# Zero halves for q and v in the first batch of a banded attention with a gated feed-forward, and its buffers moved

## Chip, cores and metric

The kernel runs on one core of one Trainium2 chip. The metric is the device time of one execution in microseconds (us), as a median of three runs. An execution that the hardware profiler took supplies the rows below.

## What is computed

Four batches, eight heads, 768 positions, head size 64. Attention looks at a window of 128 positions back and at 4 sink positions; its output, 3072 tokens of 512 features, goes through a gated feed-forward (512 to 1536 to 512):

```python
scores = scale * np.matmul(q, k.transpose(0, 1, 3, 2))
rel = pos[:, None] - pos[None, :]
in_window = (rel >= 0) & (rel < int(window))
keep = (pos[None, :] < int(n_sink)) | in_window
scores = np.where(keep, scores, -1000000000.0)
a = softmax(scores)                       # over the last axis
x = (a @ v), heads side by side           # 3072 x 512
gate = 1.0 / (1.0 + np.exp(-(x @ w_gate)))
return (gate * (x @ w_val)) @ w_out
```

All in 32-bit floats. The weights come in as 64-bit floats and are turned into two fp32r parts (high and low) on the chip.

## The kernel before, in words

**Units.** Attention works in units: one head and one group of 128-row query tiles. Batch 0 has two groups of three tiles (T = 3), so units u = 0 to 7 (group 1) and 8 to 15 (group 2); batches 1 to 3 have three groups of two tiles. Units of three tiles are called plain: scores and P times v are one fp32 matmul each (two records and four passes of the array), while T = 2 units split into fp32r parts.

**A plain unit** (`attend`, L795). Loads of k, q and v (`load`, L768); for each tile a score matmul (`qk`), a mask and row maximum on VectorE (`top`), an exponential with row sums on ScalarE; then row sums and their reciprocal (`guard`), normalisation of P on GpSimd, ScalarE or VectorE, a copy of the sink columns into `psk`, three transposes on TensorE, a copy into `wt` (the turned weights), two selects on GpSimd that cut the window's triangles, and P times v (`pv`) into one bank `xr` for a pair of heads, even head on partitions 0 to 63, odd head on 64 to 127. When both are done ScalarE copies the bank into `xs`.

**Half arrays.** From unit `DUP = 4` on, q and k of a pair of heads are loaded once, one head on the upper and one on the lower 64 partitions, and a score matmul contracts over 64 rows (`rows = slice(e, e + D)`). Units 0 to 3 load q and k of one head twice, on both halves, and contract over 128 rows with half the scale. P times v of all plain units uses 64 columns of the array (`vhl()[:, l]` is 64 wide).

**Join** (L1046). After unit 7 (and 15) the sink columns are turned, copied and split into `sk`, multiplied with sink values `vsp` in four matmuls, added onto `xs` by VectorE, and written as the high and low parts `XH` and `XL`, which the feed-forward reads.

**Feed** (L1215). Tokens go in eight chunks of three tiles. For each of twelve slices f of the hidden size: 24 matmuls of 384 columns (`m`, gate and value, in program order over all f and chunks), tanh on ScalarE, product and split on VectorE, ScalarE and GpSimd, nine matmuls of 512 columns into `o0` to `o2`.

**Weights** (`decode`, L1119; `weights`, L1172). Each f needs three matrices, each loaded through a staging buffer `wst` (three of them), decoded on ScalarE and VectorE, and kept. f0 is opened by the row sums of unit 1, f1 to f11 by those of unit 7 (`GATES`, `OPEN`).

**Shared places.** `wst1` and `wst2` hold P, v and one `wt` of early units (u < 8, `EP`, `EV`, `EW`) and serve as staging only after these are done (`plan.over`). `eq` tiles in a pool "early" hold q and k for some of the first four units; later tiles of T = 2 units (`qs`, `kh`, `vhl`) take that place. The score banks of early units (`eO`) are the banks that become `o0` to `o2`; other PSUM uses share three banks `a`.

**Order.** Every operation goes through `plan.op` with a priority (u for attention; 6 + 0.3n for the n-th decoded matrix; behind all for the feed's matmuls on TensorE; ahead of all for the feed's other work), candidates of engines and estimated durations. `Plan.run` simulates and fixes the order of each engine, SP's transfer queue included. When TensorE has nothing, it puts a fill (`warm`, a 128 x 128 matmul on the identity), always before 8.5 us and later only if the estimated share of busy time of late, weighted with each operation's `busy` (0.5 for half-array scores, else 0.97), is under `FLOOR = 0.75`. In the records all of these stand at L493, so the tiles' names tell them apart.

Of the kernel before, what the change touches and what calls it, by code (L numbers as in the profile page):

```python
# [9 lines left out]
F32 = mybir.dt.float32  # L10
# [14 lines left out]
MT = ((3,),) * 8  # L25
# [6 lines left out]
SINKU = 3  # L32
DUP = 4
SCALP = -0.5
# [405 lines left out]
def kernel(  # L440
# [73 lines left out]
    def dma(prio, ns, fn, r=(), w=()):  # L514
        plan.op(prio, [("Q", 460, fn)], r, w, dma=ns)
# [52 lines left out]
    def shared(name, n2, n3):  # L568
# [9 lines left out]

    QK = shared("qkT", 256 + 3 * KW, 384 + 4 * KW)
    XR_ = shared("xr", 512, 768)  # L580
# [12 lines left out]
    OS = [ps.tile([128, 512], F32, name=f"o{i}") for i in range(3)]  # L593
    EP = [WST[2][:, i * 3 * KW : i * 3 * KW + 3 * KW] for i in range(2)]
    EV = [
        WST[1][:, 768:960].rearrange("p (l d) -> p l d", d=D),
        WST[2][:, 6 * KW : 6 * KW + 192].rearrange("p (l d) -> p l d", d=D),
    ]
    early_pool = ExitStack()
    ep = early_pool.enter_context(tc.tile_pool(name="early", bufs=1))  # L600

    class Late:
# [4 lines left out]
        def tile(self, *a, **kw):  # L607
            if self.pool is None:
                early_pool.close()
                self.pool = main.enter_context(tc.tile_pool(name="late", bufs=1))  # L610
            return self.pool.tile(*a, **kw)

    late = Late()
    NQ = 3 * KW + 384
# [152 lines left out]

    def load(u, b, h, t0, T, prev, L, vraw, qkT, plain):  # L768

        W = T * 128  # L770
        for part, src, o, n in ((0, k, (t0 - prev) * KW, L * KW), (2, q, t0 * 128, W)):
            at = 0 if part else W
            if plain and u >= DUP:
                if h % 2 == 0:
                    dma(
                        u, 1.5 * n, lambda src=src, o=o, n=n, at=at: Q.dma_start(
                            out=qkT()[:, at : at + n],
                            in_=src[b, h : h + 2, :, o : o + n].rearrange("h d n -> (h d) n"),
                        ), w=[(qkT, part)],
                    )  # L780
                continue
# [7 lines left out]
        dma(  # L789
            u, 182.0 * L, lambda: Q.dma_start(  # L790
                out=vraw(), in_=v[b, h, :, t0 - prev : t0 - prev + L]
            ), w=[vraw],
        )

    def attend(u, b, h, t0, T, XR, XS, PSK, QKT):  # L795
# [9 lines left out]
        e = (h % 2) * D  # L805
        early = u < H
        if early and u % 2:
            vraw = Tile(EV, None, F32, "eV", 2)
        else:
            vraw = tile([128, L, D], F32, "vraw", BUFS["vraw"])  # L810
        twice = u < DUP
        if not (plain and h % 2 and not twice):
            QKT[0] = (
                Tile(EQ, None, F32, "eQ", 3) if twice and u % 5 > 1 else part(T, QK, "qkT")
            )
        qkT = QKT[0]
        rows = slice(e, e + D) if plain and not twice else slice(0, 128)
        scale = SCALE * (0.5 if twice else 1.0)
        qT = lambda: qkT()[rows, 0:W]
        kTf = lambda: qkT()[rows, W : W + L * KW]  # L820
        load(u, b, h, t0, T, prev, L, vraw, qkT, plain)
        kk2, qq2 = [(qkT, 0), (qkT, 4)], [(qkT, 2), (qkT, 6)]
        if plain:
            pairs = ((qT, kTf),)
            qk_reads = [qkT]
        else:
            qs = tile([128, W], F32R, "qs", 2, late)
            kht = tile([128, 3 * KW], F32R, "kh", 4, late)
            klt = tile([128, 3 * KW], F32R, "kh", 4, late)
# [18 lines left out]
        for t in range(T):  # L848
            sc = Tile(OS, None, F32, "eO", 3) if early else tile([128, 512], F32, "a", BUFS["a"], ps)
            first = t0 + t == 0  # L850
# [10 lines left out]
            def top(t=t, sc=sc, first=first):  # L861
                if not first:
                    V.copy_predicated(out=sc()[:, 0:128], mask=tri, data=sc()[:, KW : KW + 128])
                V.tensor_tensor_reduce(
                    out=Pv()[:, t], in0=sc()[:, 0:KW], in1=am[min(t0 + t, 2)], op0=ALU.add,
                    op1=ALU.min, scale=-scale, scalar=3.0e38, accum_out=negm_all[:, at + t : at + t + 1],
                )

            def exp(t=t):
# [92 lines left out]
        if plain:  # L962
            vhl = vht = vraw
        else:
            vht = tile([128, 3, 2 * D], F32R, "vhl", 3, late)
            vhl = lambda: vht()[:, 0:L]
            copy(u, L * D, lambda: vhl()[:, :, 0:D], vraw, [vraw], [(vht, 0)], L % 2)
            rest(
                u, L * D, lambda: vhl()[:, :, D : 2 * D], vraw, lambda: vhl()[:, :, 0:D],
                [vraw, (vht, 0)], [(vht, 1)],  # L970
            )
# [8 lines left out]
        xr = XR[0]  # L980
        M = D if plain else 2 * D

# [137 lines left out]
    def decode(prio, src, hi, lo):  # L1120
# [49 lines left out]
        rest(prio, 512, flat(lo), a, flat(hi), [a, hi], [lo])  # L1170

    def weights(f, prio):  # L1172
        fs = slice(f * 128, f * 128 + 128)
        wres[f] = []
        for nm, w in (("g", w_gate), ("v", w_val)):
            hi = Fixed(wp.tile([128, NC, 128], F32R, name=f"w{nm}h{f}"))
            lo = Fixed(wp.tile([128, NC, 128], F32R, name=f"w{nm}l{f}"))
            decode(prio(), w[fs], hi, lo)
            wres[f] += [hi, lo]
        hi = Fixed(wp.tile([128, 1, DO], F32R, name=f"woh{f}"))  # L1180
        lo = tile([128, 1, DO], F32R, "wlo", BUFS["wlo"])
        pr = prio()
        decode(pr, w_out[fs], hi, lo)
        dma(
            pr, 728.0, lambda: Q.dma_start(out=wol_d[f], in_=lo()[:, 0].bitcast(F32)), [lo], [(WOL, f)]
        )
        wres[f].append(hi)

    def feed(ci, g, parts):
# [13 lines left out]
        for j, acc in enumerate(O):  # L1203
            ot = (
                part(2, QK, "qkT") if ci == len(MT) - 1 and j == 2
                else tile([128, DO], F32, "w2", BUFS["w2"])
# [189 lines left out]
```

## Time and profile before

| | |
|---|---|
| median of 3 runs | 776.95 us (776.75 to 776.95) |
| the profiled execution's own time | 776.84 us |
| its span, first to last instruction | 775.1 us |
| TensorE busy | 761.6 us, 98% |
| VectorE, ScalarE, GpSimd busy | 440.0, 413.8, 385.8 us |
| granted TensorE clock, mean | 0.998 |

The span is what the trace shows; the 1.7 us beside it lie around the first and last instruction. A busy TensorE only means that some matmul was in flight: matmuls overlap, so costs are read from start to start.

### The profile page before, as it was taken

The page shows a single profiled execution, that of the slowest core. Times are in us where ns is not written, and L with a number is a line of the kernel's source. Part 1 is how long each engine was busy: PE and PEld are TensorE (multiplying, and loading weights), DVE is VectorE, ACT ScalarE, POOL GpSimd, SP SyncE. Part 2 cuts the span into 40 slices and gives each one's busy share as a digit, 9 for nine tenths or more (in the row PEclk, how much of TensorE's full clock was granted, in tenths as well). Part 3 has the DMA queues.
Part 4 walks back from the last instruction along what each step waited for, and adds up shares of the span by engine and source line. Part 5 has one row for each costly group of instructions (what it writes and reads, how often), then busy time and mean ns, then how long its engine had stood idle before and what let it go on. Part 6 is the DMA issues. An engine that isn't in the chain of part 4 may idle for free.

```text
span 775.1 us, 13683 instructions
## 1 busy us (share of the span) xinstructions
PE 761.6 (98%) x4184; PEld 689.9 (89%) x4184; DVE 440.0 (57%) x1398; ACT 413.8 (53%) x1222; POOL 385.8 (50%) x521
## 2 busy tenths in 40 slices
PE   8999999999999999999999999999999999999996
PEld 6577779999999999999999999999999999999995
DVE  5878888978885688938820578836831310100001
ACT  5776778877776676836721586735741321121111
POOL 3567658877786675825721477824731321112110
PEclk9999999999999999999999999999999999999999
DMA  6568788563433443523431235432401211121111
GB/s 174 163 220 279 247 277 261 159 190 109 128 111 103 118 122 100 145 63 124 113 89 44 93 104 147 115 96 85 114 29 49 64 51 42 47 67 59 45 41 59
DMA packets 63444, 90.05 MB, mean 116 GB/s; under 512 B 9220, under 2 KB 40964, under 8 KB 63364
## 3 DMA queue, kind: packets, MB, share of 16 engines
q1 hardware_dynamic: 63360, 89.10, 39.0%
q8 instruction: 35, 0.57, 0.3%
q14 instruction: 45, 0.37, 0.1%
q10 hardware_dynamic: 4, 0.00, 0.0%
HBM read 79.63 MB, written 9.44 MB: 115 GB/s over the span
## 4 chain that ended last, share of the span: by engine, by line
PE 94%; SPq 2%; DVE 1%; DMA 1%; POOL 1%; issue 0%; ACT 0%; DVEq 0%; POOLq 0%
PE m L493 52%; PE o L493 26%; PE a L493 16%; SPq L493 2%; DMA w<-in_v_sink_dram 1%; DVE a L493 0%; DVE P L493 0%; DVE wst L493 0%; POOL vsp L493 0%; POOL kh L493 0%; POOL wst L493 0%; POOL wt L493 0%; DVE gl L493 0%; DVE xr L493 0%; DVE kh L493 0%
## 5 line engine op out<-in xcount | busy, mean ns | idle before, releaser
L493 DVE SCALAR_TENSOR_TENSOR th<-th,m 128x384 f32<-128x384 f32 x96 | 52.9, 552 | 216.9 <-PE m L493 216.5
L493 POOL TENSOR_TENSOR gl<-th,gh 128x384 fp32r<-128x384 f32 x64 | 65.6, 1025 | 213.5 <-ACT gh L493 210.0
L493 PE MATMUL m<-XH,wgh 128*128 128x384 f32 x384 | 132.6, 345 | 0.0
L493 PE MATMUL m<-XH,wvh 128*128 128x384 f32 x384 | 131.4, 342 | 0.0
L493 POOL TENSOR_SCALAR_AFFINE_SELECT wt<-wt 128x512 fp32r<-128x512 f32 (+3 forms) x172 | 107.2, 625 | 46.5 <-DVE wt L493 33.3
L493 PE MATMUL m<-XH,wvl 128*128 128x384 f32 x384 | 129.4, 337 | 0.0
L493 PE MATMUL m<-XL,wvh 128*128 128x384 f32 x384 | 129.1, 336 | 0.0
L493 PE MATMUL m<-XH,wgl 128*128 128x384 f32 x384 | 129.0, 336 | 0.0
L493 PE MATMUL m<-XL,wgh 128*128 128x384 f32 x384 | 128.9, 336 | 0.0
L493 ACT CAST gh<-th 128x384 fp32r<-128x384 f32 x83 | 42.6, 513 | 153.3 <-DVE th L493 153.0
L493 PE MATMUL o<-woh,gh 128*128 128x512 f32 x288 | 117.1, 407 | 0.0
L493 PE MATMUL o<-woh,gl 128*128 128x512 f32 x288 | 113.5, 394 | 0.0
L493 PE MATMUL o<-wol,gh 128*128 128x512 f32 x288 | 112.7, 391 | 0.0
L493 ACT ACTIVATE P<-P,negm_all 128x132 f32<-128x132 f32 x180 | 72.5, 403 | 21.1 <-DVE negm_all L493 19.5
L493 ACT ACTIVATE th<-m 128x384 f32<-128x384 f32 x96 | 46.9, 489 | 67.0 <-PE m L493 66.2
L493 PEld LDWEIGHTS m<-XH,wvh 128*128 128x128 f32 x384 | 72.1, 188 | 4.4 <-issue 1.5
L493 PEld LDWEIGHTS m<-XH,wgh 128*128 128x128 f32 x384 | 72.2, 188 | 3.3 <-issue 2.5
L493 PEld LDWEIGHTS m<-XL,wvh 128*128 128x128 f32 x384 | 72.2, 188 | 2.7
L493 PEld LDWEIGHTS m<-XL,wgh 128*128 128x128 f32 x384 | 72.3, 188 | 0.7
L493 PEld LDWEIGHTS m<-XH,wgl 128*128 128x128 f32 x384 | 72.1, 188 | 0.0
L493 PEld LDWEIGHTS m<-XH,wvl 128*128 128x128 f32 x384 | 72.1, 188 | 0.0
L493 PEld LDWEIGHTS o<-woh,gl 128*128 128x128 f32 x288 | 54.0, 188 | 13.5 <-DVE gl L493 0.3
(135 smaller groups left out, 1445.2 us busy)
## 6 DMA issues: line engine op xcount, KB each, us to landing
wol<-wol_d SPq DMA_DIRECT2D x96, 256.0 KB, 2.7
qkT<-in_k_dram SPq DMA_DIRECT2D x100, 99.0 KB, 2.6
qkT<-in_q_dram SPq DMA_DIRECT2D x144, 64.0 KB, 2.3
wst<-in_moe_w_gate_dram SPq DMA_DIRECT2D x12, 512.0 KB, 4.9
wst<-in_moe_w_val_dram SPq DMA_DIRECT2D x12, 512.0 KB, 3.7
wst<-in_moe_w_out_dram SPq DMA_DIRECT2D x12, 512.0 KB, 4.1
out_dram<-w SPq DMA_DIRECT2D x23, 256.0 KB, 2.1
vraw<-in_v_dram SPq DMA_DIRECT2D x52, 96.0 KB, 2.2
```

Of the source, the lines that this page charges most:

```text
L493: return lambda *a, **kw: tc.keep_in_program_order(op(*a, **kw))
```

## The change

q of a plain head is loaded alone into one half of a tile `qz` whose other half stays zero; k of a pair is loaded once on 128 partitions; the score matmul contracts over 128 rows. v of a head fills 64 of 128 columns of a tile `vz`, zeros in the rest, so P times v uses 128 columns, and the odd head adds onto what the even head wrote (`start` only for the even head). There are two `qz` and two `vz` for each parity, zeroed once at the start by GpSimd and VectorE. k tiles come from three places for all units.

`EP` (two P) and `EW` (one turned-weights tile) get places of their own in the early pool and serve all of batch 0 (u < 16). The three staging buffers are staging from the start. The weights of f10 and f11 lie in the early pool's place and wait until all early tiles are done (`LATE`, `plan.over`). T = 2 tiles `qs`, `kh`, `vhl` lie in the normal pool.

The first join has priority 4 in place of 7 (`AHEAD`) and takes its banks from the score banks `eO`; units 8 and 9 score there too (`MORE`). The planner's estimates of plain matmuls drop from 60 + 2n to 15 + 1.7n, and their `busy` is 0.97.

```diff
-DUP = 4
+AHEAD = 3.0
+MORE = 10
+LATE = 10
@@
-    QK = shared("qkT", 256 + 3 * KW, 384 + 4 * KW)
+    NQ = 256 + 3 * KW
+    raw = const.tile([128, 3 * NQ], F32, name="qkT")
+    QK = [raw[:, i * NQ : i * NQ + NQ] for i in range(3)]
@@
-    EP = [WST[2][:, i * 3 * KW : i * 3 * KW + 3 * KW] for i in range(2)]
-    EV = [
...
-    ]
@@
-    EQ = [ep.tile([128, NQ], F32, name=f"eq{i}") for i in range(3)]
-    for tag, n in (("qs", 2), ("kh", 4), ("vhl", 3)):
-        for i in range(n):
-            plan.over[tag, i] = {("eQ", 0), ("eQ", 1), ("eQ", 2)}
-    EW = [WST[1][:, 0:768].rearrange("p (z t y x) -> p z t y x", z=1, t=3, y=2)]
-    plan.over["wst", 1] = {("eW", 0), ("eV", 0)}
-    plan.over["wst", 2] = {("eP", 0), ("eP", 1), ("eV", 1)}
+    QZ = [[ep.tile([128, 384], F32, name=f"qz{z}{i}") for i in range(2)] for z in range(2)]
+    VZ = [[ep.tile([128, 4, 128], F32, name=f"vz{z}{i}") for i in range(2)] for z in range(2)]
+    for i in range(2):
+        for z in range(2):
+            nc.gpsimd.memset(QZ[z][i][D - z * D : 2 * D - z * D], 0.0)
+        for z in range(2):
+            nc.vector.memset(VZ[z][i][:, :, D - z * D : 2 * D - z * D], 0.0)
+    EP = [ep.tile([128, 3 * KW], F32, name=f"ep{i}") for i in range(2)]
+    EW = [ep.tile([128, 1, 3, 2, 128], F32, name="ew")]
+    EARLY = {("eW", 0), ("eP", 0), ("eP", 1)} | {(f"{n}{z}", i) for n in ("qz", "vz") for z in range(2) for i in range(2)}
+    for f in range(LATE, NF):
+        for n in ("wgh", "wgl", "wvh", "wvl", "woh"):
+            plan.over[f"{n}{f}_", 0] = set(EARLY)
@@ def load
+        e = (h % 2) * D
+        vsrc = v[b, h, :, t0 - prev : t0 - prev + L]
+        if qz:
+            if h % 2 == 0:
+                dma(
+                    u, 1.5 * L * KW, lambda: Q.dma_start(
+                        out=qkT()[:, 0 : L * KW],
+                        in_=k[b, h : h + 2, :, (t0 - prev) * KW : (t0 - prev + L) * KW].rearrange(
+                            "h d n -> (h d) n"
+                        ),
+                    ), w=[qkT],
+                )
+            dma(
+                u, 0.75 * W, lambda: Q.dma_start(
+                    out=qz()[e : e + D, 0:W], in_=q[b, h, :, t0 * 128 : t0 * 128 + W]
+                ), w=[qz],
+            )
+            dma(
+                u, 182.0 * L, lambda: Q.dma_start(out=vt()[:, 0:L, e : e + D], in_=vsrc), w=[vt]
+            )
+            return
@@ def attend
-        early = u < H
+        early = u < 2 * H
...
-        if not (plain and h % 2 and not twice):
-            QKT[0] = (
-                Tile(EQ, None, F32, "eQ", 3) if twice and u % 5 > 1 else part(T, QK, "qkT")
-            )
+        if not (plain and z):
+            QKT[0] = Tile(QK, None, F32, "qkT", 3)
...
-            pairs = ((qT, kTf),)
-            qk_reads = [qkT]
+            pairs = ((lambda: qz(), lambda: qkT()[:, 0 : L * KW]),)
+            qk_reads = [qkT, qz]
...
-            sc = Tile(OS, None, F32, "eO", 3) if early else tile([128, 512], F32, "a", BUFS["a"], ps)
+            sc = Tile(OS, None, F32, "eO", 3) if u < MORE else tile([128, 512], F32, "a", BUFS["a"], ps)
...
-                u, [("PE", 60 + 2 * n if plain else 20 + 2 * mac(n), qk)], qk_reads, [sc, (P, t)],
-                busy=0.5 if plain and not twice else 0.97,
+                u, [("PE", (15 + 1.7 * n if plain else 20 + 2 * mac(n)), qk)], qk_reads, [sc, (P, t)],
...
-            a = (xr()[e : e + D] if plain else acc())[:, 0 : Z * W].rearrange("p (z x) -> p z x", z=Z)
+            a = (xr if plain else acc)()[:, 0 : Z * W].rearrange("p (z x) -> p z x", z=Z)
...
-                    start=i == 0, stop=i == len(blocks) - 1, skip_group_check=True,
+                    start=i == 0 and not (plain and z), stop=i == len(blocks) - 1, skip_group_check=True,
...
-                u, [("PE", 60 + sum(2 * n for *_, n in blocks), pv)], [vht, wt], [(xr, h % 2)]
+                u, [("PE", 15 + sum(1.7 * n for *_, n in blocks), pv)], [vht, wt], [xr]
@@ def join
-        ts = tile([128, 512], F32, "a", BUFS["a"], ps)
+        first = u == H - 1
+        bank = (
+            lambda: Tile(OS, None, F32, "eO", 3) if first
+            else tile([128, 512], F32, "a", BUFS["a"], ps)
+        )
+        u -= AHEAD if first else 0
+        ts = bank()
...
-                sp = tile([128, 512], F32, "a", BUFS["a"], ps)
+                sp = bank()
@@ def weights
+    def home(shape, name, f):
+
+        if f < LATE:
+            return Fixed(wp.tile(shape, F32R, name=name))
+        return tile(shape, F32R, name + "_", 1, late)
```

## Rows read from the trace of the kernel before

**Rows 1.** Busy time by stretch: PE, PEld, DVE, ACT, POOL, PEclk, DMA share, GB/s

```profile
8.00:48.73 40.73, 36.26 (x195) 24.86 (x193) 29.22 (x126) 30.59 (x106) 22.65 (x35) 1.00 0.67 200
48.73:150.00 101.27, 101.27 (x521) 83.42 (x521) 91.01 (x222) 78.62 (x198) 71.14 (x85) 1.00 0.76 244
150.00:400.00 250.00, 249.68 (x1438) 232.40 (x1437) 186.61 (x634) 166.96 (x538) 162.00 (x221) 1.00 0.43 119
```

**Rows 2.** Instructions on tile ident, PE, 8 to 48.7 us (ns min/median/max; first, last)

```profile
L493 PE MATMUL m<-ident x40: 272/275/377, 8.9 to 47.9; 128*128 128x128 f32 x40
```

**Rows 3.** Timeline of PE (start us, us) around one score tile, dense stretch

```profile
63.91 0.70 PE L493 MATMUL a<-qkT 64*128 64x260 f32 x2
64.55 0.44 PE L493 MATMUL m<-XH,wgh 128*128 128x384 f32 x1
```

**Rows 4.** Timeline around the first join, and the feed's first matmul

```profile
42.40 0.44 PE L493 MATMUL a<-sk,vsp 96*128 96x384 f32 x1
...
44.97 0.44 PE L493 MATMUL a<-sk,vsp 96*128 96x384 f32 x1 [0.49 <-ACT xr L493]
...
45.25 1.06 PE L493 MATMUL m<-ident 128*128 128x128 f32 x8
...
46.08 0.44 PE L493 MATMUL a<-sk,vsp 96*128 96x384 f32 x1
...
47.58 0.87 DVE L493 TENSOR_TENSOR XL<-xr,XH 128x384 fp32r<-128x384 f32 x1
...
48.73 0.44 PE L493 MATMUL m<-XH,wgh 128*128 128x384 f32 x1
```

**Rows 5.** Timeline of PE in the head: units 3 and 4

```profile
14.63 1.34 PE L493 MATMUL o<-eq 128*128 128x132 f32 x6 [1.48 <-DMA eq<-in_q_dram]
15.81 0.49 PE L493 MATMUL a<-ident,wst 128*128 128x128 f32 x3
...
18.02 1.36 PE L493 MATMUL o<-qkT 64*128 64x132 f32 x6
19.31 1.30 PE L493 MATMUL a<-wt,wst 128*64 128x256 f32 x6
```

**Rows 6.** Instructions on tiles qkT and vraw, PE, 48.7 to 122 us

```profile
L493 PE MATMUL a<-qkT x35: 379/379/483, 48.4 to 108.2; 64*128 64x260 f32 x35
...
L493 PE MATMUL a<-wt,vraw x56: 272/326/430, 52.1 to 121.0; 128*64 128x256 f32 x28, 128*64 128x128 f32 x28
```

**Rows 7.** Timeline of PE: two score tiles of a pair of heads

```profile
78.45 0.71 PE L493 MATMUL a<-qkT 64*128 64x260 f32 x4
```

**Rows 8.** Timeline of PE: one unit's P times v, dense stretch

```profile
52.06 1.51 PE L493 MATMUL a<-wt,vraw 128*64 128x256 f32 x8
53.51 0.44 PE L493 MATMUL m<-XH,wvh 128*128 128x384 f32 x1
```

**Rows 9.** Timeline of SP's transfer queue, its first two issues

```profile
0.82 1.21 SPq L493 DMA_DIRECT2D qkT<-in_k_dram  x2
```

**Rows 10.** Waits of PE: us in total, times, longest

```profile
PE o L493 <- DMA eq<-in_q_dram: 2.2, 2, 1.5
```

**Rows 11.** Timeline: unit 7's last exponential and its normalisation

```profile
31.35 0.41 ACT L493 ACTIVATE wst<-wst,negm_all 128x132 f32<-128x132 f32 x1
...
37.74 1.03 POOL L493 TENSOR_TENSOR wst<-wst,rs 128x396 f32<-128x396 f32 x1
```

**Rows 12.** Timeline of DVE, its first instruction

```profile
0.93 0.22 DVE L481 MEMSET negm_all<- 128x192 f32 x1 [0.93 <-PEq L1355]
```

**Rows 13.** Timeline: casts of f10's and f11's gate weights, f11's first matmul

```profile
132.89 0.62 ACT L493 CAST wgh<-w 128x512 fp32r<-128x512 f32 x1
...
141.99 0.61 ACT L493 CAST wgh<-w 128x512 fp32r<-128x512 f32 x1
...
145.55 0.33 PE L493 MATMUL m<-XH,wgh 128*128 128x384 f32 x1
```

**Rows 14.** Timeline of PE: its first fills

```profile
1.68 4.21 PE L493 MATMUL m<-ident 128*128 128x128 f32 x18 [1.68 <-POOL ident masks.py:199]
```

More of the change, by code (lines that the diff above doesn't have):

```diff
@@ L593 @@
     OS = [ps.tile([128, 512], F32, name=f"o{i}") for i in range(3)]
-    EP = [WST[2][:, i * 3 * KW : i * 3 * KW + 3 * KW] for i in range(2)]
-    EV = [
-        WST[1][:, 768:960].rearrange("p (l d) -> p l d", d=D),
-        WST[2][:, 6 * KW : 6 * KW + 192].rearrange("p (l d) -> p l d", d=D),
-    ]
     early_pool = ExitStack()
-    ep = early_pool.enter_context(tc.tile_pool(name="early", bufs=1))
+    ep = early_pool.enter_context(tc.tile_pool(name="early", bufs=1, side="right"))
     class Late:
@@ L609, in tile @@
                 early_pool.close()
[L610 removed]
+                self.pool = ctx.enter_context(tc.tile_pool(name="late", bufs=1, side="right"))
             return self.pool.tile(*a, **kw)
     late = Late()
[L614 to L621 removed]
+    QZ = [[ep.tile([128, 384], F32, name=f"qz{z}{i}") for i in range(2)] for z in range(2)]
[11 more added lines that the diff above has]
+            plan.over[f"{n}{f}_", 0] = set(EARLY)
     for i in range(3):
@@ L766, in sinks, with load @@
         )
-    def load(u, b, h, t0, T, prev, L, vraw, qkT, plain):
+    def load(u, b, h, t0, T, prev, L, vt, qkT, qz):
         W = T * 128
+        e = (h % 2) * D
[19 more added lines that the diff above has]
+            return
         for part, src, o, n in ((0, k, (t0 - prev) * KW, L * KW), (2, q, t0 * 128, W)):
             at = 0 if part else W
[L773 to L779, printed above, removed]
-                    )
-                continue
             for i in range(2):
@@ L788, in load @@
                 )
[L789 to L793, printed above, removed]
+        dma(u, 182.0 * L, lambda: Q.dma_start(out=vt(), in_=vsrc), w=[vt])
     def attend(u, b, h, t0, T, XR, XS, PSK, QKT):
@@ L805, in attend @@
         e = (h % 2) * D
-        early = u < H
-        if early and u % 2:
-            vraw = Tile(EV, None, F32, "eV", 2)
-        else:
-            vraw = tile([128, L, D], F32, "vraw", BUFS["vraw"])
-        twice = u < DUP
-        if not (plain and h % 2 and not twice):
-            QKT[0] = (
-                Tile(EQ, None, F32, "eQ", 3) if twice and u % 5 > 1 else part(T, QK, "qkT")
-            )
-        qkT = QKT[0]
[L817 to L821, printed above, removed]
+        early = u < 2 * H
+        z = h % 2
+        qz = Tile(QZ[z], None, F32, f"qz{z}", 2) if plain else None
+        if plain:
+            vt = Tile(VZ[z], None, F32, f"vz{z}", 2)
+        else:
+            vt = tile([128, L, D], F32, "vraw", BUFS["vraw"])
+        vraw = lambda: vt()
+        if not (plain and z):
+            QKT[0] = Tile(QK, None, F32, "qkT", 3)
+        qkT = QKT[0]
+        load(u, b, h, t0, T, prev, L, vt, qkT, qz)
         kk2, qq2 = [(qkT, 0), (qkT, 4)], [(qkT, 2), (qkT, 6)]
         if plain:
-            pairs = ((qT, kTf),)
-            qk_reads = [qkT]
-        else:
-            qs = tile([128, W], F32R, "qs", 2, late)
-            kht = tile([128, 3 * KW], F32R, "kh", 4, late)
-            klt = tile([128, 3 * KW], F32R, "kh", 4, late)
+            pairs = ((lambda: qz(), lambda: qkT()[:, 0 : L * KW]),)
+            qk_reads = [qkT, qz]
+        else:
+            qT = lambda: qkT()[:, 0:W]
+            kTf = lambda: qkT()[:, W : W + L * KW]
+            qs = tile([128, W], F32R, "qs", 2)
+            kht = tile([128, 3 * KW], F32R, "kh", 4)
+            klt = tile([128, 3 * KW], F32R, "kh", 4)
             kh, kl = (lambda t=t: t()[:, 0 : L * KW] for t in (kht, klt))
@@ L962, in attend @@
         if plain:
-            vhl = vht = vraw
+            vhl = vht = vt
         else:
-            vht = tile([128, 3, 2 * D], F32R, "vhl", 3, late)
+            vht = tile([128, 3, 2 * D], F32R, "vhl", 3)
             vhl = lambda: vht()[:, 0:L]
-            copy(u, L * D, lambda: vhl()[:, :, 0:D], vraw, [vraw], [(vht, 0)], L % 2)
+            copy(u, L * D, lambda: vhl()[:, :, 0:D], vraw, [vt], [(vht, 0)], L % 2)
             rest(
                 u, L * D, lambda: vhl()[:, :, D : 2 * D], vraw, lambda: vhl()[:, :, 0:D],
-                [vraw, (vht, 0)], [(vht, 1)],
+                [vt, (vht, 0)], [(vht, 1)],
             )
@@ L980, in attend @@
         xr = XR[0]
-        M = D if plain else 2 * D
         blocks = []
@@ L1175, in weights @@
         for nm, w in (("g", w_gate), ("v", w_val)):
-            hi = Fixed(wp.tile([128, NC, 128], F32R, name=f"w{nm}h{f}"))
-            lo = Fixed(wp.tile([128, NC, 128], F32R, name=f"w{nm}l{f}"))
+            hi = home([128, NC, 128], f"w{nm}h{f}", f)
+            lo = home([128, NC, 128], f"w{nm}l{f}", f)
             decode(prio(), w[fs], hi, lo)
             wres[f] += [hi, lo]
-        hi = Fixed(wp.tile([128, 1, DO], F32R, name=f"woh{f}"))
+        hi = home([128, 1, DO], f"woh{f}", f)
         lo = tile([128, 1, DO], F32R, "wlo", BUFS["wlo"])
@@ L1204, in feed @@
             ot = (
-                part(2, QK, "qkT") if ci == len(MT) - 1 and j == 2
+                Tile(QK, None, F32, "qkT", 3) if ci == len(MT) - 1 and j == 2
                 else tile([128, DO], F32, "w2", BUFS["w2"])
```

2 lines of the change are left out of this document (1 added, 1 removed).

## Prediction

> **What bounds the kernel now.** I read the stages first: busy time of each engine in three stretches. From 48.73 us, where the first feed-forward matmul starts, TensorE has no idle time to 150 us (101.27 of 101.27) and practically none to 400 us, while VectorE is busy 90% (91.01 of 101.27) before 150 us and 75% after [rows 1]. So behind 48.73 us the end moves with TensorE's work, one for one, provided decoded weights arrive. Ahead of it TensorE worked 36.26 of 40.73 us, and of that 20 fills (40 records, one fill is two; 0.21 us a fill, worked out below) were for nothing [rows 1, 2]: 4.5 us idle plus 4.2 us of fills, 8.7 us to be had in the head. The head is a chain of units, not a full engine: VectorE is busy 72% there, ScalarE 75%. So the change can act in two places: the cost of a half-array matmul behind 48.73 us, and the moment at which the feed starts.
>
> **Scores on the full array.** In the dense stretch a score tile on 64 rows occupies TensorE from 63.91 to 64.55 us, 0.64 us [rows 3]. Its 260 columns in four passes at 2.4 GHz are 0.433 us, so 0.21 us are lost inside the block. No full-array fp32 score stands in that stretch, so the cost after is bounded: at worst the same 0.21 (if the loss belongs to fp32 beside fp32r), at best nothing. The nearest row is a run of four full-array fp32 fills between two fp32r matmuls, 45.25 to 46.08 us: 0.83 us, against 4 x 128 x 4 / 2.4 = 0.85 [rows 4]. Nothing is lost there, and in the head three full-array tiles of a unit take 1.18 us, three half ones 1.29 [rows 5]. I take 0.20 us a block. Behind 48.4 us there are 35 records, 17 tiles (two records each) and half of one [rows 6], in 13 blocks by the timeline: 9 of one tile, 3 of two, and one special.
>
> The special one has four records, so two tiles, and takes 0.71 us, as a block of one tile does with 0.70 [rows 3, 7]: heads of a pair, on opposite halves of the rows, ran at the same time. The Trainium skill (TensorE: Matmul & The Clock Gate, Part 3, packing small matmuls) says just that: matmuls with small contractions placed on different row groups run concurrently; the trace agrees in this block. It speaks against zero halves: if all 12 remaining pairs overlapped, the change would lose some 12 x 0.43 = 5 us. In these rows 1 block of 13 does. So the loss is 0.87 - 0.64 = 0.2 us, and scores bring 12 x 0.2 - 0.2 = **2.2 us** (bounds -0.2 to 2.5).
>
> **P times v on 128 columns.** A unit's block stands from 52.06 to 53.51 us, 1.45 us [rows 8]; its 768 columns in four passes are 1.28. The 0.17 should go by the same row of fills; seven such units lie behind 48.73 us (56 records, eight each [rows 6]): **1.2 us** (bounds 0 to 1.3). The odd head adding zeros onto the even head's rows is ordered behind it on one engine and costs nothing.
>
> **The head.** First, loads. The first four units issue 20 transfers, and SP needs 1.21 us for two [rows 9], so unit 3's are out only after 12 us; TensorE waited 2.2 us for the q of units 2 and 3 [rows 10]. After, k comes by pairs and q once: 10 transfers, 6 us. I take the 2.2 us. Later each pair has five transfers for four, six more issues in all, hidden since no unit waits for loads after that. v lands in pieces of 256 bytes; P times v comes some 8 us behind the load, which covers it.
> Second, TensorE's own blocks, which stand nearly back to back behind 18 us [rows 5]: units 4 to 7 lose 1.29 - 1.18 = 0.11 each, eight P times v 0.17 each: 1.8 us.
> Third, unit 7. Its last exp starts at 31.35 and takes 0.4, but its normalisation starts at 37.74 us [rows 11]: six us, in which VectorE and ScalarE decode f0's second and third weights, which had to wait for the one staging buffer that early tiles left free. With P, v and turned weights in places of their own all three staging buffers are free from the start and that decode falls into the gaps from 16 us on. Of the 6 us I take 2.5, since the decode must still be done by the same engines.
> Fourth, the join. Its first sink matmul is at 42.40, the second only at 44.97, waiting for ScalarE to free an "a" bank; the feed then waits for XL, whose second column group starts at 47.58 us [rows 4]. With banks of its own, and priority 4 in place of 7 ahead of the decodes, I take 1.5 us; join work of units 5 to 7 that it now precedes is needed by the join anyway.
> Against it: eight memsets. VectorE's of 192 columns takes 0.22 us [rows 12], so four of 256 about 1.2; GpSimd's four of 384 I bound by the same row, 0.9 at 0.22 each and 1.8 in proportion. The masks' chain behind them has slack on VectorE, as the first matmul that spreads the scalars stands behind fills; I charge 0.8 us (bounds 0 to 3.0, both one after the other).
> Sum: -2.2 - 1.8 - 2.5 - 1.5 + 0.8 = **-7.2 us**: the feed starts at 41.5.
>
> **What is given back.** Group 2 had 13 of its 48 score records, one P times v and two transposes done before 48.4 us [rows 6], some 4.5 us. With a shorter head half of that moves behind the feed's start: **+2.2**. And weights: f11's first cast is at 141.99 and takes 0.61, its low part, by XL's 0.87 for 384 columns [rows 4], 1.2 for 512, so it is ready at 143.8; TensorE first uses them at 145.55 us [rows 13]. Margin 1.7 us only, with VectorE 90% busy. TensorE would be there some 10 us earlier, decoding some 7: I charge **+0.8** with attention of batch 1 filling the rest.
> The new wait is that f10 and f11 take the early tiles' place and so wait for unit 15, whose last P times v record is at 121.0 [rows 6]. Behind the wait stand six casts on ScalarE and their low parts on GpSimd; f10's first cast was at 132.89 [rows 13], so 12 us of margin; it costs nothing unless group 2 slips. Fills fall away as the planner counts these matmuls as full; nothing else waits for them. T = 2 units lose the wait for the early q/k place; they are not late then.
>
> Sum: -2.2 - 1.2 - 7.2 + 2.2 + 0.8 = **-7.6 us** on the profiled execution's 776.84 us (span 775.1 and 1.7 around it; the median is 0.1 above): **769.2 us**.
>
> **Rivals.**
> 1. Decoding bounds the stretch to 145 us. For: VectorE at 90%, the small margin at f11. Against: the head has 28% of VectorE idle, so work can move forward. If decoding moves by nothing, only 1.7 us are gained (775.1); if by half of 7.2, 5.3 us (771.5). Middle 773.5, chance 0.2.
> 2. The head closes up wholly: fills and idle time of 8.7 us go, plus 3.4 of blocks and 1.8 in the head, less 1: 764. For: three staging buffers and freed banks feed every engine there. Against: the unit's latency remains. Chance 0.15.
> 3. The change does not do what it says on the array: full-array fp32 loses the same between fp32r. Then the 3.4 us and the head's 1.8 stay and the overlap's 0.2 is lost as before: of the 7.6 us 5.2 go, 774.4. For: no row shows the case. Against: the fills. Chance 0.1.
> 4. Slower: the clock in the head. The planner drops its fills since it takes these blocks as full; if TensorE, idle between units, falls from 2.4 to 1.2 GHz, the eight units' 21 us of matmuls (a unit's 1.09 of scores and 1.07 of P times v in four passes, and its transposes) double, and 8.7 us of fills and idle time take up the first part. For: the first nine fills, after idle, took 4.21 us, 0.47 each against 0.21 later [rows 2, 14], the lower level. Against: granted clock 1.00 in all stretches, also where TensorE idled 1.48 us in one piece [rows 1, 5]. Price +12.5 on 769.2: 781.7; it decides from about 9 us of such extra time. Chance 0.05.
>
> **Numbers.** The forecast holds 0.5, from 766.5 to 771.5. Rivals 1 to 3 set the range's ends: 763.5 to 774.4. Within 0.2% (1.6 us, about what a measurement of this kernel can tell from no change) needs rival 1 at its worst: 0.05. Slower 0.04, faster 0.91.
>
> **What would show it.** Score blocks of one tile near 0.44 to 0.50 us between feed matmuls, P times v near 1.30; no idle for q in the first 16 us; the first XH matmul near 41 to 42 us; all wst transfers of f0 by 20 us; TensorE without idle to 400 us. Wrong would be: an idle TensorE ahead of f10 or f11, XH starting after 46 us, blocks still 0.64 us, or a granted clock below 1.00 in the head.

## The result, and the profile after

The changed kernel takes **765.13 us** (median; 764.21 to 767.5) against 776.95 (776.75 to 777.13): a ratio of 0.9853, 95% interval 0.984 to 0.9865. That is 11.8 us less; forecast were 7.6, and the result lies inside the range. Its profiled execution took 765.13 us with a span of 763.4, 11.7 below the one before.

The stages of the changed kernel, columns as in [rows 1]:

```profile
8.00:48.73 40.73, 38.22 (x222) 33.21 (x221) 36.87 (x152) 36.91 (x127) 29.14 (x41) 1.00 0.80 223
48.73:150.00 101.27, 99.92 (x546) 90.40 (x545) 91.40 (x230) 83.27 (x218) 83.45 (x96) 1.00 0.75 241
150.00:400.00 250.00, 249.29 (x1429) 232.02 (x1428) 174.84 (x582) 158.65 (x507) 159.75 (x217) 1.00 0.41 114
```

Against [rows 1] every engine did more before 48.73 us (VectorE 36.87 against 29.22, ScalarE 36.91 against 30.59), and TensorE now idles 1.35 us between 48.73 and 150, where it did not idle at all. The fills, as in [rows 2], fell from 40 records to 24:

```profile
L495 PE MATMUL m<-ident x24: 272/275/275, 8.4 to 39.4; 128*128 128x128 f32 x24
```

The timeline of TensorE around a P times v with a score tile behind it, and around a block of two score tiles, which answers to [rows 3, 8]:

```profile
52.66 0.39 PE L495 MATMUL o<-woh,gl 128*128 128x512 f32 x1
52.88 1.47 PE L495 MATMUL a<-wt,vz 128*128 128x256 f32 x8
54.19 0.60 PE L495 MATMUL a<-qkT,qz 128*128 128x260 f32 x2
...
63.70 0.39 PE L495 MATMUL o<-woh,gl 128*128 128x512 f32 x1
63.93 1.04 PE L495 MATMUL a<-qkT,qz 128*128 128x260 f32 x4
64.62 0.53 PE L495 MATMUL m<-XH,wvh 128*128 128x384 f32 x1
```

Read it by starts. P times v follows the feed matmul after 0.22 us and lasts 1.31, to 54.19. Before, it began 0.08 us late and held TensorE 1.45 us, and the first feed matmul behind it came to its successor late as well. I measured each block so, from the end of the last feed matmul's slot to the start of the second one behind it, less one slot (a feed matmul of 384 columns follows its neighbour after 0.175 us, one of 512 after 0.231): a score block of one tile fell from 0.83 to 0.44 us, one of two tiles from 1.27 to 0.87, P times v from 1.645 to 1.31.

The head of the changed kernel, timeline of ScalarE and TensorE:

```profile
8.74 1.28 ACT L495 ACT_TABLE_LOAD   x1 [8.74 <-DVE negm_all L495]
11.13 2.14 PE L495 MATMUL o<-qkT,qz 128*128 128x260 f32 x8 [1.63 <-DVE negm_all L495]
...
36.59 0.78 PE L495 MATMUL o<-sk,vsp 96*128 96x384 f32 x3
37.91 0.42 PE L495 MATMUL o<-sk,vsp 96*128 96x384 f32 x1
...
41.47 0.42 PE L495 MATMUL m<-XH,wgh 128*128 128x384 f32 x1
```

The sink matmuls of the join stand in o banks at 36.59 to 37.91 us (before, 42.40 to 46.55), and the feed starts at **41.47** us instead of 48.73. And the last two chunks' gate weights are decoded 11.1 and 13.0 us earlier than in [rows 13]:

```profile
121.76 0.62 ACT L495 CAST wgh<-w 128x512 fp32r<-128x512 f32 x1
...
128.99 0.62 ACT L495 CAST wgh<-w 128x512 fp32r<-128x512 f32 x1
```

So f11 moved by 13.0 us where the feed's start moved by 7.3: what comes between runs faster too. That is what the experiments had to explain.

Unit 7's last exponential and its normalisation, as in [rows 11]:

```profile
29.98 0.42 ACT L495 ACTIVATE ep<-ep,negm_all 128x132 f32<-128x132 f32 x1
...
31.16 0.85 POOL L495 TENSOR_TENSOR ep<-ep,rs 128x396 f32<-128x396 f32 x1 [1.42 <-DVE rs L495]
```

The normalisation stood at 37.74 us before. And the score matmuls of batch 0 that are done before the feed starts (two records a tile):

```profile
L495 PE MATMUL o<-qkT,qz x60: 276/382/589, 7.0 to 31.7; 128*128 128x260 f32 x44, 128*128 128x132 f32 x16
...
L495 PE MATMUL a<-qkT,qz x6: 381/382/384, 31.9 to 37.4; 128*128 128x260 f32 x6
```

The 60 in o banks are the 24 tiles of group 1 and, by `MORE = 10`, the six of units 8 and 9; with the three in a banks, nine tiles of group 2 are done ahead of the feed. Before, it was seven (the six and a half of the prediction end at 48.4 us, within the seventh tile).

### The profile page after: what moved, and what is told of

It reads as the page before. It is cut to its first block, busy times and chain, and to the rows that moved or that the text cites. A ratio compares the mean times of both kernels' runs of the same rounds, so it can differ in the third digit from the quotient of the medians.

```text
span 763.4 us, 13627 instructions
## 1 busy us (share of the span) xinstructions
PE 750.0 (98%) x4164; PEld 693.7 (91%) x4164; DVE 435.5 (57%) x1376; ACT 412.9 (54%) x1227; POOL 401.8 (53%) x537
## 4 chain that ended last, share of the span: by engine, by line
PE 85%; DVE 5%; ACT 4%; DMA 3%; issue 1%; SPq 0%; POOL 0%; DVEq 0%; ACTq 0%; POOLq 0%
PE m L495 49%; PE o L495 24%; PE a L495 12%; DMA wst<-in_moe_w_val_dram 2%; DVE a L495 1%; DVE w L495 1%; DMA wst<-in_moe_w_out_dram 1%; ACT a L495 1%; DMA wst<-in_moe_w_gate_dram 1%; ACT P L495 1%; DMA wol<-wol_d 0%; SPq L495 0%; ACT wst L495 0%; DVE P L495 0%; ACT ep L495 0%
## 5 line engine op out<-in xcount | busy, mean ns | idle before, releaser
L495 POOL TENSOR_TENSOR gl<-th,gh 128x384 fp32r<-128x384 f32 x67 | 68.8, 1027 | 209.8 <-ACT gh L495 205.4
L495 ACT CAST gh<-th 128x384 fp32r<-128x384 f32 x88 | 45.2, 513 | 158.5 <-DVE th L495 158.1
L495 POOL TENSOR_SCALAR_AFFINE_SELECT wt<-wt 128x512 fp32r<-128x512 f32 (+3 forms) x166 | 103.5, 624 | 43.2 <-DVE wt L495 33.2
L495 ACT ACTIVATE P<-P,negm_all 128x132 f32<-128x132 f32 x168 | 67.6, 403 | 17.7 <-DVE negm_all L495 15.9
```

Source lines behind the costliest of these rows:

```text
L495: return lambda *a, **kw: tc.keep_in_program_order(op(*a, **kw))
```

## Experiments

The kernel under test is the changed one with one thing undone, unless said otherwise. "Ratio" is against the kernel before, run on the same chip (777.03 to 777.22 us). A difference in us is one of medians, mostly from two chips; the interval of each ratio is 2 to 2.6 us wide, so one below 2 us is not clear of the noise.

### 1 to 3. Half rows, half columns, both

The order of every engine stays; only the operands of the matmuls shrink. In e2 each head again writes its own 64 partitions, with a `start` of its own.

```diff
 e1: -pairs = ((lambda: qz(), lambda: qkT()[:, 0 : L * KW]),)
     +pairs = ((lambda: qz()[e : e + D], lambda: qkT()[e : e + D, 0 : L * KW]),)
 e2: -lhsT=vhl()[:, l],
     +lhsT=vhl()[:, l, e : e + D] if plain else vhl()[:, l],
 e3: both
```

> The changed kernel with the score matmuls of batch 0 contracted over the 64 rows that hold data, in the same order on every engine. If each half-array block costs a change of array mode at both edges (0.83 us against 0.44 for one tile in the two traces), the 13 blocks behind the feed's start give back 13 x 0.39 = 5 us, less some 0.4 for each block in which two heads overlap, and the head up to 1 us: 769 to 771. Rival, the gain lies in the buffers and the array costs the same: 765 to 766.

> The changed kernel with P times v on 64 columns of the array and each head writing its own 64 partitions, in the same order. By the mode change (1.645 against 1.31 us for a unit in the two traces), 7 units behind the feed's start give 2.3 us, the nine ahead of it up to 1 us: 767.4 to 768.5. Rival, the array costs the same: 765 to 766.

> Both: scores on 64 rows and P times v on 64 columns, with all the buffers and the order of the changed kernel. By the mode change the costs add, less where a score block stands beside a P times v block: 771 to 774, so that 3 to 6 us of the gain are left for buffers, loads and join. Rival, the buffers bring the gain: 765 to 767.

Measured: half rows 780.2 us, ratio 1.0038 (1.0024 to 1.0052); half columns 766.8, 0.9861 (0.9845 to 0.9878); both 779.68, 1.0036 (1.0022 to 1.0051). The timeline of TensorE with half rows, and then with half columns:

```profile
65.53 0.70 PE L495 MATMUL a<-qkT,qz 64*128 64x260 f32 x2
66.16 0.44 PE L495 MATMUL m<-XH,wvh 128*128 128x384 f32 x1
66.44 0.33 PE L495 MATMUL m<-XL,wvh 128*128 128x384 f32 x1
```

```profile
62.14 0.34 PE L495 MATMUL m<-XH,wgl 128*128 128x384 f32 x1
62.41 1.51 PE L495 MATMUL a<-ew,vz 128*64 128x256 f32 x8
63.85 0.50 PE L495 MATMUL o<-woh,gh 128*128 128x512 f32 x1
64.19 0.39 PE L495 MATMUL o<-wol,gh 128*128 128x512 f32 x1
```

Each edit brings back its own block and leaves the other: with half rows a score tile takes 0.83 us and P times v 1.31; with half columns 0.44 and 1.64. The loss has three places: inside, 0.2 us of the score block's 0.63, and both edges. Behind the half rows the first feed matmul starts after 0.63 us and the one behind it 0.28 later, where neighbours follow after 0.175; ahead of the half columns the gap is 0.27 where 0.175 is the slot, and behind them 0.34 for 0.231. Where a P times v and a score tile stand side by side they take 1.75 us in the changed kernel, 2.13 with half rows, 2.08 with half columns and 2.28 with both: less than the two losses added, and the two blocks share an edge. So a block on part of the array costs **0.39 us** (64 rows) or **0.33 us** (64 columns), once, however many matmuls are in it: the two-tile block loses 0.40. The Trainium skill (TensorEngine Tiling (Array Packing), Key Properties) says that changing the tiling mode drains TensorE; the rows agree and give the price. The weight loads (PEld) show the edges, first around the block on half rows of [rows 3], then around one on full rows:

```profile
63.91 0.29 PEld L493 LDWEIGHTS a<-qkT 64*128 64x128 f32 x2 [0.25 <-issue]
64.54 0.19 PEld L493 LDWEIGHTS m<-XH,wgh 128*128 128x128 f32 x1 [0.34 <-issue]
```

```profile
50.20 0.36 PEld L495 LDWEIGHTS a<-qkT,qz 128*128 128x128 f32 x2
50.59 0.19 PEld L495 LDWEIGHTS o<-woh,gh 128*128 128x128 f32 x1
```

On full rows the load begins at 50.20, while the matmul ahead is in flight and 0.18 us before its own matmul at 50.38. At both edges of the half rows it begins only with its own matmul, at 63.91 and 64.54, after 0.25 and 0.34 us in which no weights were loaded.

Half columns cost 1.7 us where their blocks come to 2.3; that is not clear of the noise, so it is the timeline that shows the price. But half rows cost 15 us, not the 5 of the blocks. In the spans of the two profiles it is 12.5, and 10.1 of that lie ahead of the feed's start. Stages of this kernel:

```profile
16.00:24.00 8.00, 8.00 (x22) 5.00 (x22) 3.20 (x19) 4.69 (x19) 4.52 (x7) 0.50 0.83 272
24.00:32.00 8.00, 8.00 (x29) 5.77 (x28) 4.01 (x19) 4.62 (x15) 2.54 (x5) 0.60 0.22 58
```

The granted clock is 0.50, the level of 1.2 GHz, while TensorE shows no idle time; the feed starts at 51.55 us for 41.47. The clock fell between 12 and 14 us, after TensorE had been busy 2.72 of the 4 us from 8 to 12. That is rival 4 of the prediction, in a kernel that it was not about.

### 12. Half rows once more

Two executions of run 1 had a mean granted clock of 0.986 and 0.987 and took 777.6 and 778.9 us; three with a mean of 0.998 took 780.2 to 780.9, which does not fit a clock that costs 10 us. So the same kernel ran again.

> The kernel with scores on 64 rows once more, unchanged. In its first trace the granted clock was 0.50 for 16 us of the head, and two of its executions, with a mean granted clock of 0.986 and 0.987, took 777.6 and 778.9 us; the three with a mean of 0.998 took 780.2 to 780.9. Theory: the head runs at the lower clock in all of them and the mean of some does not show it; then a trace with a mean of 0.998 still has score matmuls of 600 to 801 ns in the head, the feed starts near 51 us, and all executions lie between 777 and 781.5. Rival: an execution with a mean of 0.998 has its head at full clock (score matmuls of at most 487 ns, feed start at 42 to 45 us) and loses the time elsewhere, with 3 us or more of TensorE idle behind the feed's start; then the clock is not what the half rows cost. If the trace again has a mean of 0.986, only the spread tells: by the theory no gap between executions of the two means beyond 4 us, by the rival a mean of 0.998 goes with a time of 770 or less in at least one.

780.24 us (1.0035; 1.0021 to 1.0048). This time the trace shows a granted clock of 1.00; the stage, and the score matmuls in it (nanoseconds, shortest, median and longest):

```profile
16.00:24.00 8.00, 8.00 (x23) 4.85 (x23) 3.72 (x24) 4.20 (x19) 3.77 (x7) 1.00 0.92 299
...
L495 PE MATMUL o<-qkT,qz x12: 424/637/800, 16.4 to 22.2; 64*128 64x260 f32 x8, 64*128 64x132 f32 x4
```

The same row of the changed kernel:

```profile
L495 PE MATMUL o<-qkT,qz x16: 276/383/385, 16.0 to 23.3; 128*128 128x260 f32 x12, 128*128 128x132 f32 x4
```

And this kernel's own, on 64 rows, behind the feed's start:

```profile
L495 PE MATMUL a<-qkT,qz x28: 378/380/484, 61.4 to 102.7; 64*128 64x260 f32 x28
```

A score matmul took 637 ns (median) where 380 to 383 is normal, just as in run 1's trace (424/637/801 in this stage): the head ran at the lower level here too, to about 31 us, and the clock's record did not show it. The feed started at 53.54. For the execution that was profiled the theory holds and the rival falls; the other four, 778.75 to 781.33 us, fit a slow head and have no trace. Durations tell the clock where its record does not.

### 4, 5 and 7. Staging, join and loads undone

```diff
 e4: -EP = [ep.tile([128, 3 * KW], F32, name=f"ep{i}") for i in range(2)]
     +EP = [WST[2][:, i * 3 * KW : i * 3 * KW + 3 * KW] for i in range(2)]
     +plan.over["wst", 2] = {("eP", 0), ("eP", 1)}
     (EW likewise in WST[1])
 e5: -AHEAD = 3.0
     +AHEAD = 0.0
     -lambda: Tile(OS, None, F32, "eO", 3) if first
     -else tile([128, 512], F32, "a", BUFS["a"], ps)
     +lambda: tile([128, 512], F32, "a", BUFS["a"], ps)
 e7: +cuts = ((0, n),) if u >= 4 else ((0, n // 2), (n // 2, n - n // 2))
     (k of a pair in four transfers, q in two, units 0 to 3; same bytes)
```

> The changed kernel with the two more P and the one more turned weights back in the second and third staging buffer, for units 0 to 7 alone, so that these two serve as staging only when those units are done. If the free staging buffers shorten the head, f0's decode moves behind unit 7 again, the feed starts 2.5 to 5 us later than 41.5 and the time is 767.5 to 770. Rival, the loads and the array shorten the head and staging is hidden: 765 to 766.

> The changed kernel with the first join at its old priority 7 and in the three shared banks. If priority and banks bring what I took for them, the feed starts 1.5 us later, near 43, and the time is 766 to 767.5. Rival, the join waits for unit 7 whatever its priority: 765.

> The changed kernel with the first four units' loads in twice the pieces, 20 transfers as before with the bytes of the changed kernel. If SP's issue time held up units 2 and 3 before, TensorE waits some 2 us for q again and the feed starts 1 to 2 us later: 766 to 767.5. Rival, the mask's chain and the table load are later than the loads in any case: 765.

| undone | time, us | ratio (interval) | feed starts | f11's first cast |
|---|---|---|---|---|
| nothing | 765.13 | 0.9853 (0.984 to 0.9865) | 41.47 | 128.99 |
| staging (e4) | 770.12 | 0.991 (0.9893 to 0.9926) | 41.81 | 133.48 |
| join (e5) | 766.74 | 0.9872 (0.9856 to 0.9887) | 42.53 | 129.39 |
| loads (e7) | 773.32 | 0.9948 (0.9934 to 0.9962) | 45.03 | 138.83 |

In these three, unlike in 1 to 3, the planner fixes every engine's order anew, so a time holds what the new order does besides. e4 came out at the upper end of the time expected, though its feed was to start 2.5 to 5 us later; e5 came out as expected; e7 did not, it was put at 766 to 767.5.

The staging places are worth 5.0 us at the end and 0.3 at the feed's start. Unit 7's last exponential and normalisation in e4:

```profile
27.75 0.41 ACT L495 ACTIVATE wst<-wst,negm_all 128x132 f32<-128x132 f32 x1 [0.25 <-DVE negm_all L495]
...
33.69 0.57 DVE L495 TENSOR_TENSOR wst<-wst,rs 128x396 f32<-128x396 f32 x1
```

Without the places the normalisation starts 5.9 us after the last exponential, much as before the change (6.4), and 2.5 us later than in the changed kernel. But from unit 7's P times v to the feed it takes 2.6 us there and 5.9 in the changed kernel, so almost nothing of it reaches the feed's start. Waits of TensorE from 48.73 to 160 us in e4 (us in total, times, longest):

```profile
PE a L495 <- DVE w L495: 1.2, 1, 1.2
PE m L495 <- DVE wvl L495: 0.7, 1, 0.7
PE m L495 <- POOL wvl L495: 0.6, 1, 0.6
PE m L495 <- DVE th L495: 0.5, 1, 0.5
```

Two of them wait for the low part of decoded weights (wvl); the longest holds a matmul of attention, which queues on VectorE behind a decode (w). In the changed kernel the largest of that stretch is a single one, for a transfer:

```profile
PE o L495 <- DMA wol<-wol_d: 0.7, 1, 0.7
```

So the staging buffers that early tiles no longer hold feed the decode of the first chunks, and it is the decode whose gain reaches the end: f11's cast is 4.5 us later without them. Loads are the dearest part: 3.6 us at the feed's start, 8.2 at the end, with f11 9.8 us later. The join gives 1.1 and 1.6, the latter not clear of the noise.

### 6, 10 and 11. A shorter head

e6 makes the exponential's table load early (a one-column `activation` behind the `negm_all` memset, ahead of everything on ScalarE), which shortens TensorE's wait of 1.63 us at 11.13 to 0.74 at 10.21. e10 adds to it two GpSimd memsets moved to VectorE and fills counted at 2.13 of their later time while the engine is taken as slow. e11 is the changed kernel itself, beside e10.

> The changed kernel with one exponential of a single column as ScalarE's first instruction, so that the load of ScalarE's table (1.28 us, at 8.74 us in the changed kernel's trace, behind the first row maximum) falls into the idle time ahead of 8 us. If the head sets the end, the feed starts 1 to 1.5 us earlier and the time is 763.6 to 764.3. Rival, decoded weights set the end (f11's are ready some 2 us ahead of their use): the feed starts earlier and the end stays, 765.

> The changed kernel with the table load early as in e6, GpSimd zeroing two q tiles in place of four (VectorE the others), and fills ahead of 7 us estimated at 2.13 times in place of 2 (0.464 us each in the trace). If the first row maximum, at 8.36 us, holds up the head, it comes 0.3 to 0.9 us earlier, the feed starts at 40 to 41 and the time is 764 to 765. Rival, ScalarE (busy 7.9 of 8 us from 24 to 32) bounds the head: feed at 41, time 765.

> The changed kernel again, beside the others: 765 us, 764 to 767.5; where the clock falls for some 3 us in the head, as in one of its four runs (767.5 at a mean clock of 0.995), about 2 us more.

e6: 765.0 (0.9845; 0.9832 to 0.9859), feed at 41.15. e10: 765.01 (0.9843; 0.983 to 0.9856), feed at 40.10. e11: 765.28 (0.9853; 0.9839 to 0.9868), feed at 40.67. Between starts of 40.1 and 41.5 the end does not move. In e10 TensorE idles 2.43 us between 48.73 and 150 us where the changed kernel idles 1.35, so most of the 1.4 us won in the head is lost there. TensorE's longest wait in this trace is for the product's low part on GpSimd, not for decoded weights:

```profile
PE o L497 <- POOL gl L497: 1.1, 1, 1.1
```

The 0.3 us that e6 wins at the start are too few to tell. No version beat the changed kernel.

### 8 and 9. Each half of the change alone

e8 keeps the new places, loads and join, and takes half rows and half columns with the planner told so (its old costs and `busy`, so that it places fills). e9 keeps the full arrays and undoes staging, join and loads together (the edits of e4, e5 and e7, and `MORE = 8`). It is not the kernel before with full arrays: the zeroing, the places of k and the late f10 and f11 stay, and both kernels have an order of their own.

```diff
 e8: e3, and
     -15 + 1.7 * n if plain else 20 + 2 * mac(n)
     +60 + 2 * n if plain else 20 + 2 * mac(n)
     +busy=0.5 if plain else 0.97,
     -15 + sum(1.7 * n for *_, n in blocks)
     +60 + sum(2 * n for *_, n in blocks)
```

> As e3_both_halves, scores on 64 rows and P times v on 64 columns with the changed kernel's buffers, loads and join, but with the old estimates (60 + 2n, and half-array scores at half weight), so that the planner puts fills where TensorE idles. In e1 and e3 the granted clock was 0.50 from 14 to 30 us, in which TensorE never idled; if that fall, and not the arrays, made some 7 of e3's 14.6 us, the clock stays at 1.00 in the head here, the feed starts at 42.5 to 44.5 and the time is 772 to 775. Rival, the clock has nothing to do with it and half arrays cost 14 us: 778 to 780.

> The changed kernel with full arrays, but staging shared as in e4, the join as in e5, the loads in 20 pieces as in e7, and units 8 and 9 scoring in the shared banks: the array part nearly alone. If arrays bring 7 us behind the feed's start wherever it starts, 768 to 771, with the feed at 46 to 47.5. Rival, weights' decoding sets the end of the first chunk once staging is shared, so that the parts taken alone (5.0, 1.6 and 8.2 us in e4, e5 and e7) add: 775 to 780.

e9: 774.61 us, ratio 0.9971 (0.996 to 0.9983; 12 runs): **2.3 us** of the 11.8. e8's executions fall into two groups: 776.25 and 776.55 us at a mean granted clock of 0.997, and 781.85, 786.8 and 787.09 at 0.992 to 0.982 (one more, of over 2 ms, is left out). Its ratio over these, 1.0127 (1.0109 to 1.0144), is mostly the clock's; with the clock up, where the profiled one lies (score matmuls of 379 ns in the head), it gains **0.6 us**, which lies within the spread of the kernel before (776.37 to 777.9). Both were expected elsewhere, e8 at 772 to 775 and e9 at 768 to 771. Each half, taken so, brings next to nothing; together they bring 11.8. The stretch from 8 to 160 us (columns as in [rows 1]), before, after, e8 and e9:

```profile
8.00:160.00 152.00, 147.53 (x770) 117.36 (x769) 128.25 (x377) 117.28 (x330) 100.61 (x129) 1.00 0.72 227
```

```profile
8.00:160.00 152.00, 147.44 (x817) 131.77 (x816) 135.18 (x404) 128.48 (x369) 120.81 (x148) 1.00 0.77 235
```

```profile
8.00:160.00 152.00, 148.96 (x763) 116.65 (x763) 125.88 (x363) 121.47 (x341) 100.47 (x129) 1.00 0.70 219
```

```profile
8.00:160.00 152.00, 145.37 (x811) 128.74 (x810) 129.46 (x384) 117.65 (x334) 107.44 (x140) 1.00 0.73 225
```

What TensorE does not use there is the idle time (152 less its busy time) and the fills, 0.105 us a record by the 0.21 us a fill of two records that the prediction worked out [rows 4]:

| | idle | fill records | idle and fills, us | feed starts | span |
|---|---|---|---|---|---|
| before | 4.5 | 40 | 8.7 | 48.73 | 775.1 |
| after | 4.6 | 24 | 7.1 | 41.47 | 763.4 |
| e8, half arrays | 3.0 | 31 | 6.3 | 46.27 | 774.5 |
| e9, arrays alone | 6.6 | 74 | 14.4 | 53.83 | 774.6 |
| e4, staging undone | 6.2 | 34 | 9.7 | 41.81 | 767.6 |
| e7, loads undone | 8.3 | 31 | 11.6 | 45.03 | 770.9 |

With half arrays TensorE is the fuller one: the new places leave it less unused than before, 6.3 us for 8.7, but the edges take the time. With full arrays alone it has time over and nothing to do: 14.4 us, against 7.1 with the new places. So I take the first to be bound by the array, the second by what reaches it. The feed's start is no measure by itself: e9 starts it 5.1 us later than the kernel before and ends 0.5 us of span earlier.

## Why the prediction came out as it did

**The size.** Forecast -7.6, measured -11.8. By its terms:

| term | forecast, us | measured, us |
|---|---|---|
| score blocks behind the feed's start | -2.2 (-0.2 to 2.5 gained) | -4.7: 9 x 0.39 + 3 x 0.40, less 0.03 for the block that overlapped |
| P times v there | -1.2 (0 to 1.3 gained) | -2.35: 7 x 0.335 |
| feed's start | -7.2 (41.5) | -7.26 (41.47) |
| group 2 given back | +2.2 | about -0.9: nine score tiles are done ahead of the feed, seven before, so two fewer are left behind it, at 0.44 |
| TensorE starved | +0.8 | about +1.7: 1.35 more idle to 150 us, 0.39 more to 400 [rows 1] |
| other blocks behind the feed's start | 0 | about +1.7: from start to start, all blocks there that are not batch 0's scores or P times v took 92.2 us before and 94.0 after |
| sum | -7.6 | -11.8, of -11.7 in the profiles |

**Right**: that the score and P times v blocks shrink, that the mode's loss does not come back on the full array (rival 3 out), that the feed would start at 41 to 42 us, that the wait for unit 15 costs nothing (its last P times v now stands at 100.64 us, f10's first cast at 121.76), and that the one overlapped block says little against zero halves (0.845 us then, 0.874 now). Its price against them, 12 pairs at 0.43, was too high: the other twelve blocks hold 15 tiles, so seven pairs, about 3 us.

**Wrong, the step "0.21 us are lost inside the block".** I timed the block from its first start to the next start, 63.91 to 64.55 [rows 3], and left out both edges: the matmul ahead has a slot of 0.175 from 63.65, so 0.085 us were lost before 63.91, and the first feed matmul behind held TensorE from 64.55 to 64.82, 0.27 for 0.175. That makes 0.39, above my upper bound; the same omission halved P times v. The fills that I took as the nearest row [rows 4] showed that full-array fp32 loses nothing, which was right, but they could not show what a half array loses. Scores and P times v together are 3.6 of the 4.2 us missed.

**Wrong, "half of that moves behind the feed's start".** Nothing of group 2's scores was given back. The change itself lets units 8 and 9 score in the o banks, and nine tiles instead of seven are done ahead of the feed, 3.1 us better than forecast. Starved time and the other blocks, 2.6 us worse than forecast, hide most of that; that the sum came nearer than its terms is luck.

**Wrong though its sum came out: the head's steps.** The feed's start of 41.5 was met to 0.03 us by parts that were missed by more, which is luck. The staging step put 2.5 us on unit 7, and unit 7 does what it says: its normalisation follows the last exponential after 1.2 us where it took 6.4 [rows 11], and undoing the places puts 2.5 us back on it (e4). What failed is the path: this moves the feed's start by 0.3 us only, and the end by 5.0. TensorE's own blocks in the head were put at 1.8; with half arrays the feed starts 4.8 us later (e8, which also places more fills). The join was put at 1.5 and gives 1.1 at the start, 1.6 at the end; the loads at 2.2 and give 3.6 and 8.2. The memsets: GpSimd's first took 0.42 us and its three others 1.34, VectorE's four 1.09, inside the bounds; the first row maximum stood only 0.1 us later. Not foreseen was the table load, 1.28 us behind that maximum, which e6 shows to cost nothing at the end. And f0's last weight transfer was waited for until 24.04 us, not 20: that sign did not come.

**Wrong, adding the parts.** The prediction adds them as if each moved the end by itself. Undone one at a time they cost 5.0 (e4), 1.6 (e5), 8.2 (e7) and 11.3 (e8, clock up): 26 us of a gain of 11.8. TensorE has to be short of work and work has to be at hand, so neither half pays alone (0.6 and 2.3).

**Rivals.** Rival 1, decoding, did not bound the gain but was the right place to look: f11's decode moved by 13.0 us, more than the head, and between 48.73 and 150 us GpSimd is busier (83.45 for 71.14) and ScalarE too (83.27 for 78.62), with VectorE as before (91.40 for 91.01). From f1's first cast to f11's it takes 87.8 us for 95.9. Rival 2, the head closing up wholly, did not happen: 2.5 us of idle time before 48.73 us and 24 fill records are left. Rival 4, the clock, does not show in the profiled execution of the changed kernel, but in runs 1, 3 and 12 and in three of e8's five executions it does, and there it turns the gain into a loss. My condition for it, fills left out, is not shown: in e3, half arrays counted as full, all executions take 779.43 us or more, but in e8, whose planner places fills for them, only two of five kept the clock.

**Open.** Why the other blocks cost 1.7 us more I have not placed; waits too short to show as idle time are one candidate. What makes the granted clock fall, and why e8 goes either way, was not tried further. About two thirds of e4's extra span is accounted for by idle time and fills (2.6 of 4.2 us); the rest is not. Half arrays in the changed kernel's own order and with the clock up were never seen: e3 lost the clock and e8 has another order. So how the 11.3 us of e8 divide between blocks and order is argued, not shown.

## What to carry to other kernels

Price a matmul block on part of the array from the feed matmul ahead of it to the second one behind, not by its own records: here a block cost 0.39 and 0.33 us, twice what it showed inside. Where the array and the supply of work limit in turn, try both parts together before dropping either, and judge a shorter head by the pace of what follows, not by its start. Compare durations of one shape between stages to see the clock, even where its record reads 1.00.

## What was not expected of the hardware

- Score matmuls on 64 rows, with TensorE at 8.00 of 8.00 us busy, ran at the lower level for 16 us and more (0.50 granted from 14 to 30 us in e1; 637 ns for 383 in e12). Against the changed kernel the feed started 10.1 and 12.1 us later. The Trainium skill (TensorE: Matmul & The Clock Gate, Part 1) ties the clock to how busy the engine has been; here an engine without idle time by the profile stood at the lower level, so the busy share of the profile did not tell it. In e1 the fall came after 2.72 us busy of the 4 from 8 to 12, yet the changed kernel, busy 2.37 of the same 4, stayed at 1.00. In e12 TensorE did not idle at all from 1.92 to 45 us, and the matmuls took the time of the lower level to about 31.
- The granted clock read 1.00 in e12 while the matmuls took the time of the lower level.
- The clock can also fall in the changed kernel's own order: in e2, whose instructions are the same up to the first P times v, it was 0.50 from 12 to 14 us, after TensorE had been busy 0.51 of the 2 us from 8 to 10. This may be what spreads the changed kernel's runs over 764.21 to 767.5 (the slowest has a mean granted clock of 0.995, the fastest 0.998); e6, whose idle time there is 0.74 us in place of 1.63, spread over 764.36 to 765.67. It is not settled.
